# Sliding-window attention and a tanh-shrink layer: even key spans of V by DMA, odd ones copied by VectorE, GpSimd's casts for the third batch moved

## Chip, cores and metric

The kernel runs on one core of a Trainium2 chip. The metric is the device time of one execution in microseconds (us). A core has TensorE (PE in the profile), VectorE (DVE), ScalarE (ACT) and GpSimd (POOL), each with its own in-order instruction stream. SyncE (SP) here only issues DMAs. GpSimd issues DMAs as well, on a queue of its own.

## What is computed

Attention over a causal window of 64 keys, for 8 batches of 8 heads with 576 positions and head size 64, and then one layer with the activation h - tanh(h). The reference, cut down:

```python
scores = scale * np.matmul(q, k.transpose(0, 1, 3, 2))     # q, k, v: (8, 8, 576, 64), float32
rel = pos[:, None] - pos[None, :]
mask = (rel >= 0) & (rel < 64)
scores = np.where(mask, scores, -1000000000.0)
attn = softmax(scores)
x = (attn @ v).transpose(0, 2, 1, 3).reshape(4608, 512)
h = x @ w_in                                               # (512, 2048)
out = (h - np.tanh(h)) @ w_out                             # (2048, 512)
```

## The kernel before

**The two halves of the work.** The 4608 tokens of the layer are taken in nine chunks of 512. For each chunk c and each of 16 tiles m of the hidden size, `hp_mm` does four matmuls with `w_in` (L383) and a tanh on ScalarE (L388), `g_sub` the subtraction on VectorE (L395, into `gT`), and `yp_mm` the matmuls with `w_out` (L407); `y_out` copies the result (L412) and stores it from SP's queue (L414). `hp_mm` for chunk 0 starts with three tiles together, first for the half of `xT` that comes first (`split`), then for the other.

**Attention.** It is taken by pairs of heads: g = 4 b + pr, with batch b and pair pr, so 32 steps g. For each g: cast q and k to bf16 (`cast`, L85), transpose them on TensorE (`tr_rows` L269, later `tr` L249), copy them out of PSUM (L83 on ScalarE, L85 on VectorE), multiply (`tile_scores` L288, later `scores` L316), exponentiate (L291, L318), mask, multiply with V (`tile_pv` L304, later `pv` L332), and normalize (L308/L310, L339/L343). `tile_scores` masks in two ways: with "hide" it adds a large negative number by two matmuls (L276) in front of each of its two groups; with "mask" VectorE multiplies the exponentials by zero or one (L295). `x_tr` transposes the result into `xT`, from which `hp_mm` reads.

**V and its windows.** A query span of 64 tokens needs its own 64 keys and the 64 before. So `vw` holds, for each span j of nine, 128 rows: rows 64 to 127 are the keys of span j, rows 0 to 63 those of span j - 1. There are two such buffers, for even and odd batches. V is loaded to `vall`, cast into `vb` (`cast_v`, L85; 72 partitions of eight tokens), and from `vb` spread over partitions by DMA. Two ways are used: `keys_v` (L165) brings 64 rows of one span, 65 KB, and then the lower half is a copy of the upper half one span on, `shift_v`; `windows_v` (L150) brings all 128 rows, 130 KB. Before the change batches 0, 1 and 2 use nine `keys_v`, some issued by GpSimd (G) and some by SP (Y), and two VectorE copies `shift_dve` of 64 x 2080 elements (L171). Batches 3 and 4 use `windows_v`, the later ones `keys_v` and DMA.

**Order.** The order on every engine is written out by hand. A prologue does batch 0's attention. Then a loop over steps h issues the layer's instructions of step h (the table `OPS`), and after them whatever was put at this step by `at(h, ...)`, so `at(39, f)` places f at step 39. `cast_pair(g, eng)` casts k and q of g on the engine eng; `VALUES[b]` has the steps of batch b's casts of V and of its windows. Loads of q, k, V and the weights are issued by GpSimd, in the order of its stream: after the windows of batch 2 (step 23) come `w_out` in two halves and q, k and V of batch 3 whole. The DMAs of GpSimd use eight completion semaphores in turn, and each instruction that issues one waits for the DMA that had its semaphore before.

Of the kernel before, what the change touches and what calls it, by code (L numbers as in the profile page):

```python
# [15 lines left out]
def kernel(  # L16
# [9 lines left out]
    nc = tc.nc  # L26
    B, H, S, D = q.shape
    NP = H // 2
    NJ = S // 64
# [32 lines left out]
    mask = ps[:, 5, 448:480].bitcast(BF16)  # L62
    hide = const.tile([128, 2, 64], BF16, name="hide")
# [7 lines left out]
    vw = [const.tile([128, NJ, H, D + 1], BF16, name=f"vw{i}") for i in range(2)]  # L71
# [74 lines left out]
    def windows_v(b, j, eng):  # L146
        if j == 0:
            keys_v(b, 0, eng)
        else:
            eng.dma_start(out=vw[b % 2][:, j].rearrange("p h c -> p (h c)"),  # L150
                          in_=vb[8 * j - 8:8 * j + 8].rearrange("p e h c -> p e (h c)"))
# [7 lines left out]
    def cast_v(b, pr, eng=nc.gpsimd):  # L159
        move(eng, vb[:, :, 2 * pr:2 * pr + 2, 0:D].rearrange("p e h d -> p h e d"),  # L160
             stage.pop((b, pr, "v")).rearrange("p h (e d) -> p h e d", d=D))

    def keys_v(b, j, eng=nc.sync):

        eng.dma_start(out=vw[b % 2][64:128, j].rearrange("p h c -> p (h c)"),  # L165
                      in_=vb[8 * j:8 * j + 8].rearrange("p e h c -> p e (h c)"))

    def shift_v(b, j0, j1, eng=nc.sync):
        lo, hi = vw[b % 2][0:64, j0 + 1:j1 + 1], vw[b % 2][64:128, j0:j1]
        if eng is nc.vector:  # L170
            eng.tensor_copy(lo, hi)  # L171
        else:
            eng.dma_start(out=lo.rearrange("p j h c -> p (j h c)"), in_=hi.rearrange("p j h c -> p (j h c)"))
# [5 lines left out]
    def load_w_in(i):  # L179
        nc.gpsimd.dma_start(out=w_in_sb[i], in_=w_in_r[:, :, 1024 * i:1024 * i + 1024])  # L180

    def w_in_tile(ki, m):
        i = m // 8
        f = 512 * (m // 4 % 2) + m % 4
        return w_in_sb[i][:, ki, f:f + 4 * 127 + 1:4]
# [38 lines left out]
    def chunk_tile(c):  # L224
        if c not in xT:
            xT[c] = xt_pool.tile([128, WPC, 2, 128], BF16, tag="xT", name="xT")
        return xT[c]
# [7 lines left out]
    def tr_heads(g, which, bank, eng):  # L235

        src = stage.pop((g, which))
        tp = ps[:, bank, :].bitcast(BF16)[:, 0:E * P].rearrange("c (e p) -> c e p", e=E)
        for e in range(E):
            for h in range(2):  # L240
                nc.tensor.transpose(tp[64 * h:64 * h + 64, e, :], src[:, h, D * e:D * e + D], ident[:P, :P])
        o = qs[g % 2] if which == "q" else kT[g % NK][:, 64:]
        move(eng, o.rearrange("c (p e) -> c p e", e=E), tp.rearrange("c e p -> c p e"))
# [29 lines left out]
    def hides(grp, banks):  # L273
        n = GROUPS[grp][1]
        for h in range(2):
            nc.tensor.matmul(ps[:, banks[h], 0:64 * n], ident, hide[:, h].unsqueeze(1).to_broadcast([128, n, 64]),  # L276
                             start=True, stop=False)

    def tile_scores(g, grp, banks, how="hide"):

        j0, n = GROUPS[grp]
        if how == "hide":
            hides(grp, banks)
        for i in range(n):
            j = j0 + i
            for h in range(2):
                r = slice(64 * h, 64 * h + 64)
                nc.tensor.matmul(ps[:, banks[h], 64 * i:64 * i + 64], kT[g % NK][r, 64 * j:64 * j + 128],  # L288
                                 qs[g % 2][r, 64 * j:64 * j + 64], start=how == "mask", stop=how == "mask" or i == n - 1)
        o = PT[g % NPT][:, j0:j0 + n].rearrange("p j (h t) -> p h j t", h=2)  # L290
        nc.scalar.activation(o, pair_of(banks)[:, :, 0:64 * n].rearrange("p h (j t) -> p h j t", t=64),  # L291
                             ACT.Exp, scale=scale)
        if how == "mask":
            p = PT[g % NPT][:, j0:j0 + n].rearrange("p j (h t) -> p (j h) t", h=2)
            nc.vector.tensor_tensor(p, p, mask_sb.unsqueeze(1).to_broadcast([128, 2 * n, 64]), ALU.mult)  # L295
# [78 lines left out]
    def hp_bank(c, m):  # L374
        return H0_BANKS[m] if c == 0 else (m + 2) % 3 if c == 1 else m % 2

    def hp_mm(c, ms, split):

        outs = [ps[:, hp_bank(c, m), :] for m in ms]
        for kis in ((0, 2), (1, 3)) if split else ((0, 1, 2, 3),):  # L380
            for m, hp in zip(ms, outs):
                for ki in kis:
                    nc.tensor.matmul(hp, w_in_tile(ki, m),  # L383
                                     chunk_tile(c)[:, :, ki % 2, 64 * (ki // 2):64 * (ki // 2) + 64],
                                     start=(ki == 0), stop=(ki == 3))
        for m, hp in zip(ms, outs):
            th = sm_pool.tile([128, TOK], F32, tag="th", name="th")
            nc.scalar.activation(th, hp, ACT.Tanh)  # L388
            HID[c, m] = hp, th
# [51 lines left out]
    def at(h, fn, *args):  # L441
        items.setdefault(h, []).append((fn, args))
# [3 lines left out]
        c, m = [OPS[i][1:] for i in range(h) if OPS.get(i, "-")[0] == "h"][-1]  # L446
        nc.gpsimd.tensor_copy(tick, gT[c][0:1, m, 0:1])  # L447

    def shift_dve(b, *js):
        for j in js:  # L450
            shift_v(b, j, j + 4, nc.vector)

    V, A, G, Y = nc.vector, nc.scalar, nc.gpsimd, nc.sync

# [19 lines left out]
        cast_v(0, pr, V)  # L474
    tile_scores(0, 0, (0, 1))
    tile_scores(0, 1, (4, 5))
    for j, eng in enumerate((G, G, G, Y, G, Y, G, Y, G)):
        keys_v(0, j, eng)
    load_w_in(0)
    for pr in range(NP):  # L480
        load_v(1, pr)
# [17 lines left out]
    tile_scores(2, 0, (0, 1), "mask")  # L499
    tile_scores(2, 1, (4, 5), "mask")  # L500
    tr_heads(3, "q", 3, A)
    shift_dve(0, 0, 4)
    hides(0, (0, 1))
    hides(1, (4, 5))
    tile_scores(3, 0, (0, 1), "hidden")
# [16 lines left out]

    at(0, lambda: nc.vector.memset(vw[1][0:64, 0], 0.0))
    at(0, lambda: nc.vector.memset(qT[1], 0.0))
    for pr, h in enumerate((0, 0, 1, 3)):
        at(h, cast_v, 1, pr, V)
    at(9, lambda: [keys_v(1, j, (G, Y)[j % 2]) for j in range(NJ)])
    at(5, cast_pair, 4, V)
    at(9, cast_pair, 5, V)
    for pr in range(NP):  # L530
        at(9, load_v, 2, pr)
# [2 lines left out]
        at(9, load, g, "q", G)  # L534
    at(16, cast_pair, 6, V)
    at(16, cast_pair, 7, V)
    at(18, shift_dve, 1, 0, 4)
    for g, t, ka, qa, a, b, eng in ((4, (10, 11, 13, 14), 6, 7, (4, 5), (6, 7), V),
                                    (5, (13, 14, 16, 17), 2, 3, (4, 5), (6, 7), V),
                                    (6, (17, 18, 20, 22), 2, 3, (4, 5), (4, 5), A),  # L540
                                    (7, (20, 22, 24, 26), 3, 3, (4, 5), (4, 5), A),
                                    (8, (31, 32, 34, 36), 3, 5, (4, 5), (4, 5), A),
                                    (9, (37, 38, 42, 44), 3, 6, (4, 5), (4, 5), A)):
        at(t[0], tr_rows, g, "k", ka, eng)
        at(t[1], tr_rows, g, "q", qa, A)
        at(t[2], tile_scores, g, 0, a, "hide" if g < 8 else "mask")
        at(t[3], tile_scores, g, 1, b, "hide" if g < 8 else "mask")
    for pr in range(NP):
        at(22 + 2 * pr, tile_pv, 4 + pr, (6, 7))
    at(27, x_tr, 1, 0, 0, 4, 3, A)  # L550
# [1 line left out]
    at(30, x_tr, 1, 1, 0, 4, 7, V)  # L552
    at(30, x_tr, 1, 1, 4, 9, 4, A)
    at(21, lambda: [cast_v(2, pr) for pr in range(NP)])
    at(21, cast_pair, 8, G)
    at(23, lambda: [keys_v(2, j, (G, Y)[j % 2]) for j in range(NJ)])
    at(33, cast_pair, 9, V)
    at(23, load_w_out, 0)
    at(23, load_w_out, 1)
    at(23, load_all, 3, "q")  # L560
    at(23, load_all, 3, "k")
    at(23, load_v_all, 3)
    at(44, cast_pair, 10, G)
    at(50, cast_pair, 11, G)
    at(39, shift_dve, 2, 0, 4)
    at(44, tile_pv, 8, (6, 7))
    at(48, tile_pv, 9, (6, 7))
    at(53, x_tr, 2, 0, 0, 4, 6, V)
    at(55, x_tr, 2, 0, 4, 9, 7, A)
    at(76, x_tr, 2, 1, 0, 4, 3, V)  # L570
# [2 lines left out]
    LOADS = {4: (75, 77, 79), 5: (106, 109, 102), 6: (140, 144, 126), 7: (0, 0, 158)}  # L573
    STEPS = {2: (0, 0, 49, 57), 3: (72, 79, 86, 93), 4: (100, 107, 114, 121), 5: (128, 135, 142, 149)}
    TURNS = {13: (97, 3, 99, 3), 15: (110, 4, 111, 3)}
    VALUES = {3: (66, 1, 71), 4: (88, 1, 93), 5: (110, 2, 120), 6: (132, 5, 150), 7: (168, 2, 175)}
    for g in range(2 * NP + 2, B * NP):
        b, pr = divmod(g, NP)
        a = STEPS[b][pr] if b in STEPS else 8 * g - 36
# [28 lines left out]
        if b > 2:  # L608
            cv, cs, ky = VALUES[b]
            at(cv + cs * pr, cast_v, b, pr)  # L610
# [16 lines left out]
    for h in range(32 * NC + 64):  # L627
        op = OPS.get(h)
        if op and op[0] == "h":
            c, m = op[1:]  # L630
            if c == 0 and m == 0:
                hp_mm(c, (0, 1, 2), True)
            elif c > 0 or m > 2:
                hp_mm(c, (m,), m == 0)
        elif op == ("y", NC - 1, M - 4):
            y_last()
        elif op and op[1:] < (NC - 1, M - 4):
            yp_mm(*op[1:])
            if op[2] % 4 == 3:
                y_out(op[1], op[2] // 4)  # L640
        for fn, args in items.pop(h, []):
            fn(*args)
        if op and op[0] == "h":
            g_sub(*op[1:])
# [30 lines left out]
```

## Time and profile before

| | us |
|---|---|
| median of 4 runs | 337.04 (336.88 to 337.54) |
| the profiled execution | 340.34 |
| its span, first to last instruction | 338.6 |
| TensorE / VectorE / ScalarE / GpSimd busy | 319.8 / 198.5 / 184.0 / 118.6 |
| DMA moved | 40.68 MB, 120 GB/s on average |

In the groups of instructions, each line has the source line, engine, operation, what is written from what, shapes and count, then busy time in us and the mean of one in ns, and the idle time of its engine before these instructions with what ended it:

```profile
L395 DVE TENSOR_TENSOR gT<-ps,th 128x512 bf16<-128x512 f32 x144 | 98.4, 689 | 72.7 <-ACT th L388 71.5
...
L85 POOL COPY vb<-vall 72x1024 bf16<-72x1024 bf16 x24 | 24.7, 1052 | 35.4 <-DMA vall<-in_v_dram 25.8
...
L85 POOL COPY kb<-kall 96x768 bf16<-96x768 bf16 x23 | 19.8, 859 | 2.5 <-DMA kall<-in_k_dram 2.5
```

A timeline line has the start in us, the duration in us, the engine, source line, operation and count, and in brackets the idle time before it and its releaser. A line of waits has who waited for whom: us in total, how many times, the longest. A row of the table of windows has the stretch and its length, the busy us (and number of instructions) of PE, PE's weight loads, DVE, ACT and POOL, the granted clock of TensorE as a share of full speed, the DMA engines' busy share, and GB/s.

### The profile page before, as it was taken

The numbers are of one execution on the slowest core, as the hardware profiler recorded it, in microseconds if no ns is written. First come the engines' busy times: TensorE is split into PE (matmuls) and PEld (weight loads), VectorE is DVE, ScalarE is ACT, GpSimd is POOL, SyncE is SP. The second block draws the span as 40 slices with busy tenths as digits, with TensorE's granted clock in tenths as the row PEclk, the third lists the DMA queues.
The fourth block names the chain that finished last, engine by engine and source line by source line (L and its number), as shares of the span: only waits on it lengthen the run. The fifth ranks groups of instructions, "written<-read, shape, count | busy, mean of one in ns | idle before, by whom it ended". The sixth has DMA issues, their size and how long they took to land.

```text
span 338.6 us, 6275 instructions
## 1 busy us (share of the span) xinstructions
PE 319.8 (94%) x2439; PEld 176.6 (52%) x2439; DVE 198.5 (59%) x335; ACT 184.0 (54%) x337; POOL 118.6 (35%) x173
## 2 busy tenths in 40 slices
PE   6769999899987999999999999999999999999996
PEld 2544565555544655555565555555555444444444
DVE  4586697983254767666676766677665444443300
ACT  3534778683553676666566666655554444444411
POOL 8837499603940725730823585400000000000000
PEclk9598999999997999999999999999999999999999
DMA  8999998996599189648693996787213200100022
GB/s 160 162 179 191 171 155 123 174 203 133 86 174 182 13 147 180 135 80 163 110 172 92 172 179 137 139 195 166 57 57 68 71 33 31 62 33 31 31 75 83
DMA packets 47318, 40.68 MB, mean 120 GB/s; under 512 B 18728, under 2 KB 40680, under 8 KB 47096
## 3 DMA queue, kind: packets, MB, share of 16 engines
q0 software_dynamic: 21536, 19.73, 39.5%
q1 hardware_dynamic: 25544, 20.25, 23.4%
q8 instruction: 19, 0.31, 0.4%
q10 hardware_dynamic: 208, 0.29, 0.3%
q14 instruction: 11, 0.09, 0.1%
HBM read 36.70 MB, written 10.62 MB: 140 GB/s over the span
## 4 chain that ended last, share of the span: by engine, by line
PE 69%; DMA 12%; DVE 7%; POOL 6%; ACT 3%; issue 2%; POOLq 0%; DVEq 0%
PE ps L407 33%; PE ps L383 27%; DMA vw<-vb 4%; DMA qall<-in_q_dram 3%; DMA wi<-in_moe_w_in_dram 3%; PE ps L332 3%; PE ps L316 3%; DVE xs L343 2%; PE ps L249 2%; DMA kall<-in_k_dram 2%; POOL vall L143 1%; DVE gT L395 1%; DVE qt L85 1%; POOL kall L96 1%; POOL qall L96 1%
## 5 line engine op out<-in xcount | busy, mean ns | idle before, releaser
L383 PE MATMUL ps<-xT,wi 128*128 128x512 bf16 x576 | 149.2, 384 | 3.4 <-DMA wi<-in_moe_w_in_dram 1.6
L407 PE MATMUL ps<-w_out_sb,gT 128*128 128x512 bf16 x560 | 141.5, 380 | 0.0
L395 DVE TENSOR_TENSOR gT<-ps,th 128x512 bf16<-128x512 f32 x144 | 98.4, 689 | 72.7 <-ACT th L388 71.5
L388 ACT ACTIVATE th<-ps 128x512 f32<-128x512 f32 x144 | 85.9, 598 | 88.6 <-PE ps L383 84.9
L383 PEld LDWEIGHTS <-wi 128*128 128x128 bf16 x576 | 60.9, 114 | 49.8 <-issue 5.9
L407 PEld LDWEIGHTS <-gT 128*128 128x128 bf16 x560 | 52.4, 98 | 53.0 <-issue 1.1
L318 ACT ACTIVATE pt<-ps 128x384 bf16<-128x384 f32 x66 | 32.3, 489 | 23.8 <-PE ps L316 23.8
L85 POOL COPY vb<-vall 72x1024 bf16<-72x1024 bf16 x24 | 24.7, 1052 | 35.4 <-DMA vall<-in_v_dram 25.8
L343 DVE TENSOR_TENSOR xs<-ps,rc 64x576 bf16<-64x576 f32 x44 | 33.2, 755 | 1.1
L412 ACT ACTIVATE ysb<-ps 128x512 f32<-128x512 f32 x35 | 21.0, 599 | 18.9 <-PE ps L407 18.8
L85 DVE COPY qt<-ps 64x576 bf16<-64x576 bf16 x18 | 13.7, 760 | 24.1 <-ACT qt L83 24.1
L332 PEld LDWEIGHTS <-pt 128*128 128x128 bf16 x198 | 16.5, 98 | 18.8 <-issue 3.5
L85 POOL COPY qb<-qall 96x768 bf16<-96x768 bf16 x23 | 19.7, 857 | 17.8 <-DVE gT L395 10.7
L332 PE MATMUL ps<-vw,pt 128*128 128x130 bf16 x198 | 22.2, 220 | 3.8 <-DMA vw<-vb 3.4
L316 PE MATMUL ps<-qt,kt 128*128 128x128 bf16 x198 | 22.0, 220 | 0.0
L85 POOL COPY kb<-kall 96x768 bf16<-96x768 bf16 x23 | 19.8, 859 | 2.5 <-DMA kall<-in_k_dram 2.5
L316 PEld LDWEIGHTS <-kt 128*128 128x128 bf16 x198 | 15.6, 99 | 9.2 <-issue 0.8
L322 DVE TENSOR_TENSOR pt<-pt,ps 128x1152 bf16<-128x1152 bf16 x22 | 16.4, 745 | 0.8 <-ACT pt L318 0.8
L83 ACT ACTIVATE kt<-ps 128x576 bf16<-128x576 bf16 x22 | 14.4, 654 | 1.9 <-PE ps L249 1.6
L291 ACT ACTIVATE pt<-ps 128x640 bf16<-128x640 f32 (+1 forms) x20 | 12.5, 647 | 2.9 <-PE ps L288 2.9
L447 POOL COPY tick<-gT 1x1 bf16<-1x1 bf16 x14 | 2.5, 179 | 28.5 <-DVE gT L395 21.3
L165 POOL DMA_DIRECT2D vw<-vb x17 | 10.1, 600 | 6.2 <-DMA wi<-in_moe_w_in_dram 2.9
(76 smaller groups left out, 214.9 us busy)
## 6 DMA issues: line engine op xcount, KB each, us to landing
out_dram<-ysb SPq DMA_DIRECT2D x35, 256.0 KB
vall<-in_v_dram POOLq DMA_DIRECT2D x5, 576.0 KB, 12.0
vw<-vb SPq DMA_DIRECT2D x39, 65.0 KB
qall<-in_q_dram POOLq DMA_DIRECT2D x4, 576.0 KB, 11.9
kall<-in_k_dram POOLq DMA_DIRECT2D x4, 576.0 KB, 10.6
kall<-in_k_dram POOLq DMA_DIRECT2D x15, 144.0 KB, 6.0
qall<-in_q_dram POOLq DMA_DIRECT2D x15, 144.0 KB, 5.7
wi<-in_moe_w_in_dram POOLq DMA_DIRECT2D x2, 1024.0 KB, 10.6
```

The lines of the kernel that those rows point to most:

```text
L83: nc.scalar.activation(o, i, ACT.Copy)
L85: eng.tensor_copy(o, i)
L316: nc.tensor.matmul(sp[:, i, :], kT[g % NK][:, 64 * j:64 * j + 128], qT[g % NR][:, :, 64 * j:64 * j + 64], start=True, stop=True)
L318: nc.scalar.activation(PT[g % NPT][:, 3 * grp:3 * grp + 3, :], sp, ACT.Exp, scale=scale)
L322: nc.vector.tensor_tensor(p, p, mask.unsqueeze(1).to_broadcast([128, 2 * NJ, 64]), ALU.mult)
L332: nc.tensor.matmul(ps[:, 5 + grp, 130 * i:130 * i + 130], PT[g % NPT][:, j, :], vw[b % 2][:, j, 2 * pr:2 * pr + 2, :], start=True, stop=True)
L343: nc.vector.tensor_tensor(xo[r, :, :, pr, :], ov[r, :, :, h, 0:D], rc[r].to_broadcast([64, 3, 3, 64]), ALU.mult)
L383: nc.tensor.matmul(hp, w_in_tile(ki, m), chunk_tile(c)[:, :, ki % 2, 64 * (ki // 2):64 * (ki // 2) + 64], start=(ki == 0), stop=(ki == 3))
L388: nc.scalar.activation(th, hp, ACT.Tanh)
L395: nc.vector.tensor_tensor(gT[c][:, m, :], hp, th, ALU.subtract)
L407: nc.tensor.matmul(yp, gT[c][:, m, s * 128:(s + 1) * 128], w_out_sb[:, m, :], start=(m == 0), stop=(m == M - 1))
L412: nc.scalar.activation(ysb, ps[:, yp_bank(c, s), :], ACT.Copy)
```

## The change

Batches 0, 1 and 2 get V differently. The five even spans j = 0, 2, 4, 6, 8 come whole by DMA with `windows_v` (j = 0 needs only its upper half). The odd spans are copied by VectorE from their neighbours: the lower half of j is the upper half of j - 1, and the upper half of j is the lower half of j + 1 (`odd_windows`). A batch so has five DMAs instead of nine, with the same bytes, and two VectorE copies of 4 x 520 elements (for batch 2, three copies: one of 4 x 520 and two of 2 x 520, the last a step later). Batch 2's five DMAs are all issued by GpSimd.

k and q of g = 8, 10 and 11, which GpSimd cast, are cast by VectorE (8 and 11) and ScalarE (10). The transposes and scores of g = 8 and 9 come one to three steps later, their products with V one step later, g = 9's cast three steps later, and the casts of batch 1's V are spread over the steps 0, 1, 3, 5. g = 5's scores are masked by VectorE's multiplication instead of by matmuls. Batch 3's casts of V are at the steps 68 to 71 and its windows at 72, instead of 66 to 69 and 71. `hp_mm` starts chunk 0 with two tiles together instead of three.

```diff
-    def shift_dve(b, *js):
-        for j in js:
-            shift_v(b, j, j + 4, nc.vector)
+    def odd_windows(b, half, j0=1, n=4):
+
+        lo, hi = vw[b % 2][0:64], vw[b % 2][64:128]
+        at_j = slice(j0, j0 + 2 * n - 1, 2)
+        if half == 0:
+            nc.vector.tensor_copy(lo[:, at_j], hi[:, j0 - 1:j0 + 2 * n - 2:2])
+        else:
+            nc.vector.tensor_copy(hi[:, at_j], lo[:, j0 + 1:j0 + 2 * n:2])
+
+    def even_windows(b, *engs):
+
+        for j, eng in zip((0, 4, 2, 8, 6), engs):
+            windows_v(b, j, eng)
...
-    for j, eng in enumerate((G, G, G, Y, G, Y, G, Y, G)):
-        keys_v(0, j, eng)
+    for j, eng in ((8, Y), (0, G), (2, G), (4, G), (6, G)):
+        windows_v(0, j, eng)
...
-    shift_dve(0, 0, 4)
+    odd_windows(0, 0)
+    odd_windows(0, 1)
...
-    for pr, h in enumerate((0, 0, 1, 3)):
+    for pr, h in enumerate((0, 1, 3, 5)):
         at(h, cast_v, 1, pr, V)
-    at(9, lambda: [keys_v(1, j, (G, Y)[j % 2]) for j in range(NJ)])
-    at(5, cast_pair, 4, V)
+    at(9, even_windows, 1, G, Y, G, Y, G)
+    at(6, cast_pair, 4, V)
...
-    at(18, shift_dve, 1, 0, 4)
+    at(18, odd_windows, 1, 0)
+    at(18, odd_windows, 1, 1)
...
-                                    (8, (31, 32, 34, 36), 3, 5, (4, 5), (4, 5), A),
-                                    (9, (37, 38, 42, 44), 3, 6, (4, 5), (4, 5), A)):
+                                    (8, (34, 35, 37, 39), 3, 5, (4, 5), (4, 5), A),
+                                    (9, (38, 39, 42, 44), 3, 6, (4, 5), (4, 5), A)):
...
-        at(t[2], tile_scores, g, 0, a, "hide" if g < 8 else "mask")
-        at(t[3], tile_scores, g, 1, b, "hide" if g < 8 else "mask")
+        at(t[2], tile_scores, g, 0, a, "hide" if g in (4, 6, 7) else "mask")
+        at(t[3], tile_scores, g, 1, b, "hide" if g in (4, 6, 7) else "mask")
...
-    at(21, cast_pair, 8, G)
-    at(23, lambda: [keys_v(2, j, (G, Y)[j % 2]) for j in range(NJ)])
-    at(33, cast_pair, 9, V)
+    at(31, cast_pair, 8, V)
+    at(23, even_windows, 2, G, G, G, G, G)
+    at(36, cast_pair, 9, V)
...
-    at(44, cast_pair, 10, G)
-    at(50, cast_pair, 11, G)
-    at(39, shift_dve, 2, 0, 4)
-    at(44, tile_pv, 8, (6, 7))
-    at(48, tile_pv, 9, (6, 7))
+    at(46, cast_pair, 10, A)
+    at(53, cast_pair, 11, V)
+    at(39, odd_windows, 2, 0)
+    at(39, odd_windows, 2, 1, 1, 2)
+    at(40, odd_windows, 2, 1, 5, 2)
+    at(45, tile_pv, 8, (6, 7))
+    at(49, tile_pv, 9, (6, 7))
...
-    VALUES = {3: (66, 1, 71), 4: (88, 1, 93), 5: (110, 2, 120), 6: (132, 5, 150), 7: (168, 2, 175)}
+    VALUES = {3: (68, 1, 72), 4: (88, 1, 93), 5: (110, 2, 120), 6: (132, 5, 150), 7: (168, 2, 175)}
...
-                hp_mm(c, (0, 1, 2), True)
-            elif c > 0 or m > 2:
+                hp_mm(c, (0, 1), True)
+            elif c > 0 or m > 1:
```

## Prediction, made before the changed kernel was run

> **What bounds the kernel now.** I read the page first, then TensorE's waits, then the table of windows, then GpSimd's timeline backwards from the longest wait.
>
> ```profile
> PE 319.8 (94%) x2439; PEld 176.6 (52%) x2439; DVE 198.5 (59%) x335; ACT 184.0 (54%) x337; POOL 118.6 (35%) x173
> ...
> PEclk9598999999997999999999999999999999999999
> ```
>
> TensorE is the bound, 319.8 of 338.6 us, so only what it waits for, and its clock, can give time. Each digit of the clock row is a fortieth, 8.5 us: after the start there is one dip, the 7 of the slice from 101.6 us.
>
> ```profile
> PE ps L332 <- DMA vw<-vb: 3.4, 1, 3.4
> PE ps L383 <- DMA wi<-in_moe_w_in_dram: 1.6, 1, 1.6
> ...
> PE ps L383 <- DVE gT L395: 1.4, 3, 0.8
> ...
> PE ps L269 <- POOL kb L85: 0.7, 1, 0.7
> ```
>
> The longest wait (99.9 + 0.2 to 103.47 us) is the product with V of batch 3, held by one of the transfers that fill `vw`. It costs twice: the clock after it is granted at 0.59 for 4 us, a loss of 0.41 x 4 = 1.6 us.
>
> ```profile
> 100.00:104.00 4.00, 0.62 (x6) 0.34 (x4) 1.67 (x3) 0.66 (x2) 0.00 (x0) 0.98 1.22 257
> 104.00:108.00 4.00, 4.00 (x19) 2.02 (x18) 2.86 (x4) 1.52 (x3) 0.00 (x0) 0.59 1.02 201
> ```
>
> So 3.4 + 1.6 = 5.0 us hang on when batch 3's V reaches `vw`. GpSimd's timeline tells why it is late:
>
> ```profile
> 36.84 0.55 POOL L165 DMA_DIRECT2D vw<-vb  x1 [2.92 <-DMA wi<-in_moe_w_in_dram]
> 38.10 0.55 POOL L165 DMA_DIRECT2D vw<-vb  x1 [0.70 <-DMA kall<-in_k_dram]
> 39.58 0.71 POOL L143 DMA_DIRECT2D vall<-in_v_dram  x1 [0.93 <-DMA qall<-in_q_dram]
> ...
> 47.97 4.03 POOL L85 COPY vb<-vall 72x1024 bf16<-72x1024 bf16 x4
> 51.94 0.82 POOL L85 COPY kb<-kall 96x768 bf16<-96x768 bf16 x1
> 52.71 0.82 POOL L85 COPY qb<-qall 96x768 bf16<-96x768 bf16 x1
> 53.48 2.92 POOL L165 DMA_DIRECT2D vw<-vb  x5
> 56.39 1.49 POOL L188 DMA_DIRECT2D w_out_sb<-in_moe_w_out_dram  x2
> ...
> 82.00 1.05 POOL L85 COPY vb<-vall 72x1024 bf16<-72x1024 bf16 x1 [5.67 <-DMA vall<-in_v_dram]
> 82.99 0.82 POOL L85 COPY kb<-kall 96x768 bf16<-96x768 bf16 x1
> 83.76 3.04 POOL L85 COPY vb<-vall 72x1024 bf16<-72x1024 bf16 x3
> ```
>
> V of batch 3 lands at 82.0. It is queued behind `w_out`, q and k, and these behind GpSimd's casts and window transfers. Meanwhile the DMA engines run half empty:
>
> ```profile
> 52.00:54.00 2.00, 1.34 (x15) 0.76 (x13) 0.95 (x3) 1.60 (x4) 2.00 (x3) 1.00 0.60 86
> 54.00:56.00 2.00, 1.90 (x23) 1.10 (x22) 1.22 (x3) 1.85 (x4) 2.00 (x5) 1.00 0.72 130
> 56.00:58.00 2.00, 2.00 (x23) 1.06 (x22) 1.30 (x4) 1.78 (x4) 2.00 (x4) 1.00 0.90 143
> 58.00:60.00 2.00, 2.00 (x15) 0.99 (x13) 1.96 (x4) 1.90 (x4) 2.00 (x3) 1.00 0.66 84
> ```
>
> The last column is GB/s: 111 on average over 8 us, where 66 to 76 us has 205. That is 8 x (205 - 111) / 205 = 3.7 us of transfer time lost.
>
> **Start (0 to 25 us).** Batch 0's windows: nine transfers of 65 KB become one of 65 and four of 130, so bytes are equal; GpSimd issues 4 instead of 6, 2 x 0.57 us less. In the program's list of waits its DMAs share eight completion semaphores in turn, so each waits for the one eight before it; the first `w_in` load at 14.16 waited 0.77 us so. Two DMAs fewer put it behind an earlier one (k of g=2, landed by 11.9): issue at 9.67 + 4 x 0.57 = 12.0. The transfers are in order, so only unused DMA time counts: 15 to 18 us has 159, 110 and 141 GB/s against about 190 later, 160 KB short, 0.85 us. TensorE waits 1.6 us for `w_in`; take 0.8 us gain (0 to 1.6). The odd copies need all even windows, so the first product with V can start only after the second copy, near 18.5 instead of 18.23; it is hidden, since `xT` is ready at 24.5 and its first half at 22.7. `hp_mm` with two tiles instead of three lets the first tanh start four matmuls earlier; nothing waits there but a 0.8 us wait for gT at 33.9; taken as 0.
>
> A rule against row: the Trainium skill (TensorE: Matmul & The Clock Gate, Part 1) has the clock halve after an idle window of about 3.4 us. The trace halves it after less: 1.6 us of waiting, with thin work before it, and 25 to 29 us is granted 0.57. By the rule a shorter wait removes that 1.7 us; by the row it may well stay, so I take 0.
>
> **GpSimd's queue (31 to 56 us).** The windows of batch 1 are 3 instead of 5 issues on GpSimd. In the row above the last two are held by the rotation until 36.84 and 38.10, and the V loads of batch 2 behind them until 39.58. With two fewer these loads stand two places further back: the first waits for `w_in`'s second half (36.8, less 0.8) and the last for the load that lands at 40.6, less 0.8. From there 8 issues x 0.64 = 5.1 us: about 45.0 instead of 47.97, 3.0 us (1 to 3). Then 4.0 us casts of V, no k and q casts (-1.54), five window issues (2.8): `w_out` is issued at about 52 instead of 56.4, 4.5 us earlier. The DMA time to be filled is 3.7 us, so V of batch 3 lands 3.5 us earlier, at 78.5 (2 to 4). A k cast no longer stands between its V casts (-0.8): all cast at 82.5 instead of 86.8. SP's half of batch 3's windows stands behind two stores of y, the second out at 83.6, whose time is TensorE's. So the windows come 3.2 us earlier, plus what TensorE gains.
>
> A rule that speaks against this: the Trainium skill (SBUF — State Buffer, SBUF: two separate sides) says a DMA issued by GpSimd cannot get its descriptors written while VectorE runs a two-port copy. Batch 2's windows all move to GpSimd. The row: 17 such issues take 551/571/957 ns (min, median, max), those five 0.56 to 0.64, and land after 3.5 to 4.0 us. By the row the move costs nothing; by the rule up to a copy (0.70) an issue, 3.5 us. I keep the row for the middle and 2 us for the range.
>
> **The compute engines (31 to 76 us).**
> - Batch 2's window copies on VectorE: two took 2.46 us beside GpSimd's k and q casts, the pair of batch 1 1.33 us without them. Without casts: -1.1 us. TensorE's waits there are 0.4 (gT, 62.8) and 0.3 us (xs, 65.1). The new copies have the same elements in runs of 520 with gaps; no row shows gaps. Bounds: as before, 0.70 each, or one element a cycle, by the 64x520 memset at 0.49, so 2.0 each. Runs are long and rows even: 0.7.
> - k and q of g=8 from GpSimd to VectorE: +0.70, in a VectorE idle of 1.8 us (54.8); TensorE's wait of 0.7 us for kb goes, and its next is for `xT` (53.0): 0.4 gained.
> - g=10 to ScalarE: two copies, nearest row 0.84 (96x768 from fp32), lower bound 0.65; +1.7 us in a stretch where ScalarE waits 1.4 and 0.5 us for TensorE. g=11 to VectorE: +0.70 at about 69 us, where VectorE is 97% busy; up to 0.7 lost.
> - g=5's mask by multiplication: four matmuls fewer (1152 columns; 512 take 0.216 us: -0.5 us on TensorE), 0.49 + 0.42 more on VectorE, ahead of gT and of the window copies, whose product with V follows at 44.3: up to 0.9 lost.
> - Steps of g=8, g=9, their products with V and the last cast of g=8: later by 1 to 3 steps, free as long as batch 2 is not what the end waits for.
>
> Sum for TensorE ahead of 100 us: 0.8 + 0.4 + 0.5 + 0.7 = 2.4, less a likely half of the added 0.7 + 0.9 + 0.5: about 1.4 us (-1 to 2.5).
>
> **The sum.** TensorE would reach the product at 100.1 - 1.4 = 98.7; the windows are there at 103.5 - 3.2 - 1.4 = 98.9. The wait is nearly gone and the clock stays: 4.6 + 1.6 = 6.2 us off the profiled execution, which took 340.3 us (span 338.6 and 1.7 around it): 334.1. The median of the runs is 337.0, 3.3 less. The only places where it can have lost less are such waits and clock dips, so I suppose that an ordinary run has some 2 to 3 of the 5.0 us. That gives 337.0 - 1.4 - 2.2 = 333.4.
>
> **Rivals.**
> 1. The stall stays: the last window on SP took 12.6 us in the chain (90.82 to 103.47) beside batch 4's k, q and V loads, which are issued right behind the windows (91.4 to 94.9) and so come earlier too. For: 201 to 257 GB/s there. Against: all shift alike. Only 1.4 us remain: 335.6. Chance 0.2.
> 2. The added VectorE and ScalarE work (3 us) lands on TensorE and eats the gain: within 0.2% of before, 337.0. For: VectorE 87% busy from 54 to 66 us. Against: TensorE had 3.4 us to spare before the stall. Chance 0.08.
> 3. Slower: the odd copies of batch 2 at step 39 block VectorE. All five even windows are on one queue; if GpSimd is not early, the last is issued at 54.8 and lands by the worst row (9.8 us) at 64.6, five us after the copies' turn at 59.6; gT stands behind them, and TensorE has two banks. It decides once the last even window lands after about 63, when more than the stall's 3.4 us is lost. Then 5.0 - 1.8 (the part of the stall an ordinary run has): about 340. Chance 0.12.
> The main case has 0.6.
>
> **Numbers.** Within 0.2% (0.7 us) is about what a measurement of this kernel cannot tell from no change. Faster 0.60 + 0.20 = 0.80, same 0.08, slower 0.12. The range goes from the full profile gain (337.0 - 6.4 = 330.6) to no change (337.0), which leaves out rival 3 and half of rival 2.
>
> **What would show it.** Right: batch 3's first V cast near 78.5 us, `w_out` issued near 52, 52 to 60 us near 200 GB/s, no wait of L332's product over 1 us, no 7 in the clock row, window copies of 0.7 us. Wrong: V cast of batch 3 still at 82 (the queue was not the cause); TensorE waiting for gT or xs between 55 and 80 us (rival 2); VectorE idle before the odd copies (rival 3).

## The result and the profile after

| | before | after |
|---|---|---|
| median of the runs side by side, us | 336.55 (56 runs, 333.9 to 340.98) | 334.40 (37 runs, 332.5 to 336.89) |
| ratio after / before | | 0.9948 [0.9933, 0.9962] |
| the profiled execution, us | 340.34 | 336.89 |
| its span | 338.6 | 335.2 |

By the ratio the change makes the kernel 0.52% faster, 1.75 us (1.3 to 2.3) of 336.55; the two medians are 2.15 us apart, inside that interval. The prediction took off 3.6 us. Both profiled executions are near the longest of their kernels' runs, so the difference of the two spans is not the gain; they show where time goes within each.

The page of after, its TensorE totals and clock row:

```profile
PE 318.1 (95%) x2435; PEld 176.5 (53%) x2435; DVE 199.3 (59%) x342; ACT 185.4 (55%) x339; POOL 110.9 (33%) x163
...
PEclk9569899999999999999999999999999999999999
```

The 7 at 101.6 us is gone. A new 8 stands in the fifth slice (33.5 to 41.9 us). The waits of TensorE in after (total us, how often, the longest):

```profile
PE ps L383 <- DMA wi<-in_moe_w_in_dram: 2.3, 2, 1.8
...
PE ps L383 <- DVE gT L395: 1.0, 2, 0.8
...
PE ps L407 <- ACT ysb L412: 0.3, 1, 0.3
```

The wait of L332's product for `vw`, 3.4 us before, is not in the list at all. The longest wait of the layer is now for the second half of `w_in`, 1.8 us. The table of windows of after confirms both stretches (columns as before: PE, PE's loads, DVE, ACT, POOL, clock, DMA share, GB/s):

```profile
36.00:38.00 2.00, 0.24 (x4) 0.13 (x2) 0.67 (x1) 0.98 (x2) 0.00 (x0) 1.00 1.31 243
...
40.00:42.00 2.00, 2.00 (x11) 1.02 (x10) 1.61 (x5) 1.67 (x4) 2.00 (x4) 0.50 0.94 147
...
52.00:54.00 2.00, 2.00 (x19) 1.09 (x17) 1.97 (x5) 1.67 (x4) 2.00 (x5) 1.00 0.76 62
54.00:56.00 2.00, 1.85 (x19) 1.15 (x19) 1.51 (x4) 1.33 (x4) 2.00 (x3) 1.00 0.93 164
56.00:58.00 2.00, 1.61 (x21) 0.86 (x19) 1.75 (x5) 2.00 (x5) 1.69 (x3) 1.00 0.86 145
58.00:60.00 2.00, 2.00 (x27) 1.33 (x26) 1.61 (x3) 1.72 (x4) 0.00 (x0) 1.00 1.08 168
100.00:104.00 4.00, 4.00 (x32) 2.24 (x29) 2.80 (x5) 3.16 (x7) 0.00 (x0) 1.00 1.09 184
104.00:108.00 4.00, 4.00 (x34) 2.39 (x33) 2.93 (x5) 2.19 (x5) 0.00 (x0) 1.00 0.56 119
```

At 100 to 108 us TensorE is now busy throughout at full clock. From 52 to 60 us the DMA engines move (62 + 164 + 145 + 168) / 4 = 135 GB/s instead of 111, not the 200 that the prediction hoped for. Between 36 and 38 us TensorE waits for `w_in`, and from 39.5 us on the clock is halved.

GpSimd's timeline of after, the lines that answer to the chain shown of before:

```profile
38.11 0.71 POOL L143 DMA_DIRECT2D vall<-in_v_dram  x1 [5.01 <-DMA wi<-in_moe_w_in_dram]
...
46.78 4.03 POOL L85 COPY vb<-vall 72x1024 bf16<-72x1024 bf16 x4
...
51.71 2.12 POOL L150 DMA_DIRECT2D vw<-vb  x4
53.79 1.49 POOL L188 DMA_DIRECT2D w_out_sb<-in_moe_w_out_dram  x2
...
80.21 4.04 POOL L85 COPY vb<-vall 72x1024 bf16<-72x1024 bf16 x4 [2.86 <-DMA vall<-in_v_dram]
84.54 0.60 POOL L165 DMA_DIRECT2D vw<-vb  x1 [0.30 <-POOL vb L85]
```

`w_out` is issued 2.6 us earlier than before (53.79 for 56.39), V of batch 3 lands 1.8 us earlier (80.21 for 82.0) and its windows start 2.6 us earlier (84.54 for 87.10), since no k cast lies between its four casts. But the first profile of before began late: in a second one (e5, below) the same three stand at 55.34, 80.84 and 85.94, and after is ahead of them by only 1.6, 0.6 and 1.4 us.

To see where TensorE gains or loses, I read from each trace when VectorE begins the subtraction (L395) of the first, ninth, 32nd and 39th tile of the layer, in us from the start of the span; the last column goes from the 39th tile to the last instruction. The first tile needs the first half of `w_in`, the ninth the second half; the 32nd comes after all of batches 1 and 2's work, the 39th after the product that stalled. Experiments are listed too, and told below.

| us | 1st tile | 9th | 32nd | 39th | 9th to 32nd | 32nd to 39th | 39th to end |
|---|---|---|---|---|---|---|---|
| before, first profile | 29.56 | 41.41 | 74.83 | 111.03 | 33.42 | 36.20 | 227.6 |
| before again (e5) | 27.04 | 40.36 | 73.77 | 105.22 | 33.41 | 31.45 | 227.6 |
| after | 27.82 | 41.30 | 75.80 | 106.80 | 34.50 | 31.00 | 228.4 |
| after, g=5 by matmuls (e4) | 26.73 | 41.44 | 74.33 | 105.66 | 32.89 | 31.33 | 228.4 |
| after, V first (e8) | 28.50 | 41.48 | 74.35 | 105.34 | 32.87 | 30.99 | 228.4 |
| before, V first (e3) | 25.95 | 39.39 | 72.97 | 103.96 | 33.58 | 30.99 | 227.6 |
| casts part alone (e2) | 26.82 | 40.28 | 72.78 | 104.54 | 32.50 | 31.76 | 227.8 |
| windows part alone (e1) | 26.95 | 39.00 | 75.03 | 106.02 | 36.03 | 30.99 | 228.1 |

Four things stand in it. The column from the 32nd to the 39th tile shows the stall: 36.20 - 31.00 = 5.2 us in the two profiles at hand. The column before it shows the work between: 34.50 in after, of which about 1.7 us is the half clock from 39.5 to 42.9 us (3.4 x 0.5), so 32.8 without it, against 33.4. The ninth tile starts between 39.0 and 41.6 us, with no order between kernels that have the old windows and those that have the new. And the last column shows a loss of 0.8 us behind the 39th tile, in each of the three profiles of after and its near kin. Of it 0.3 us comes with the casts part: the wait for ScalarE's copy of y (L412) in the list above, which before and e1 do not have. The other 0.5 us comes with the windows part, behind all work: from the end of the last copy (L425) to the last instruction it is 2.8 us in every profile with the old windows and 3.3 us in every one with the new, where SyncE runs out its last waits. Why, the runs do not show.

### The profile page after: what moved, and what is told of

Read it like the earlier page. It is cut to its first block, busy times and chain, and to the rows that moved or that the text cites. A ratio compares the mean times of both kernels' runs of the same rounds, so it can differ in the third digit from the quotient of the medians.

```text
span 335.2 us, 6239 instructions
## 1 busy us (share of the span) xinstructions
PE 318.1 (95%) x2435; PEld 176.5 (53%) x2435; DVE 199.3 (59%) x342; ACT 185.4 (55%) x339; POOL 110.9 (33%) x163
## 4 chain that ended last, share of the span: by engine, by line
PE 75%; DMA 9%; DVE 7%; ACT 4%; issue 2%; POOL 2%; POOLq 0%; DVEq 0%; ACTq 0%
PE ps L407 34%; PE ps L383 30%; DMA wi<-in_moe_w_in_dram 7%; PE ps L332 3%; PE ps L316 3%; DVE xs L343 2%; PE ps L249 2%; DMA kall<-in_k_dram 2%; DVE qt L85 2%; DVE gT L395 1%; ACT qt L83 1%; PE ps L422 1%; ACT pt L318 1%; POOL vall L143 1%; PE ps L349 1%
## 5 line engine op out<-in xcount | busy, mean ns | idle before, releaser
L395 DVE TENSOR_TENSOR gT<-ps,th 128x512 bf16<-128x512 f32 x144 | 98.5, 690 | 68.1 <-ACT th L388 66.7
L412 ACT ACTIVATE ysb<-ps 128x512 f32<-128x512 f32 x35 | 21.0, 600 | 18.9 <-PE ps L407 18.5
L85 POOL COPY qb<-qall 96x768 bf16<-96x768 bf16 x20 | 16.6, 832 | 25.5 <-DMA qall<-in_q_dram 25.5
L332 PEld LDWEIGHTS <-pt 128*128 128x128 bf16 x198 | 16.5, 98 | 15.3 <-DVE pt L322 0.8
L332 PE MATMUL ps<-vw,pt 128*128 128x130 bf16 x198 | 22.0, 220 | 0.4 <-DVE pt L322 0.4
L85 POOL COPY kb<-kall 96x768 bf16<-96x768 bf16 x20 | 16.6, 829 | 3.1 <-DMA kall<-in_k_dram 3.1
L96 POOL DMA_DIRECT2D qall<-in_q_dram x15 | 9.9, 660 | 7.5 <-DMA wi<-in_moe_w_in_dram 6.2
L83 ACT ACTIVATE qt<-ps 64x576 bf16<-64x576 bf16 x18 | 11.5, 638 | 1.0 <-PE ps L249 0.9
```

The source lines that it names most:

```text
L83: nc.scalar.activation(o, i, ACT.Copy)
L85: eng.tensor_copy(o, i)
L332: nc.tensor.matmul(ps[:, 5 + grp, 130 * i:130 * i + 130], PT[g % NPT][:, j, :], vw[b % 2][:, j, 2 * pr:2 * pr + 2, :], start=True, stop=True)
L395: nc.vector.tensor_tensor(gT[c][:, m, :], hp, th, ALU.subtract)
L412: nc.scalar.activation(ysb, ps[:, yp_bank(c, s), :], ACT.Copy)
```

## The experiments

The theory after the result: the gain is mostly the stall of batch 3's V, which GpSimd's freed queue takes away; of what TensorE was to gain ahead of it little came. Rivals: the new windows at the start bring the gain; or TensorE's gain was there and the work added to VectorE and ScalarE (g=5's mask, the casts) ate it. In these kernels only order, engine and way of transfer change.

### e1: the windows part alone

Before, with the even windows by DMA and the odd ones copied, all else as it was:

```diff
+    def odd_windows(b, half, j0=1, n=4):
...
-    for j, eng in enumerate((G, G, G, Y, G, Y, G, Y, G)):
-        keys_v(0, j, eng)
+    for j, eng in ((8, Y), (0, G), (2, G), (4, G), (6, G)):
+        windows_v(0, j, eng)
...
+    at(9, even_windows, 1, G, Y, G, Y, G)
+    at(18, odd_windows, 1, 0)
+    at(18, odd_windows, 1, 1)
+    at(23, even_windows, 2, G, G, G, G, G)
+    at(39, odd_windows, 2, 0)
+    at(39, odd_windows, 2, 1, 1, 2)
+    at(40, odd_windows, 2, 1, 5, 2)
```

> The kernel before with only the windows part: even spans by DMA, odd ones copied, batches 0 to 2; casts and steps stay. Queue theory (the time comes from batch 3's V reaching vw earlier): GpSimd's stream is shorter by the two issues and the rotation alone, about 1.2 us by the changed kernel's first V cast of batch 2 (46.78 for 47.97), so about 1 us faster than before (ratio 0.997), a wait on vw of about 2 us left in the profile. Engine theory (the gain is TensorE's own, from the copies and the earlier start): most of the change's gain is here, ratio 0.995 to 0.996, whatever the wait on vw does.

Measured: 0.9986 [0.9965, 1.0007] of before, no change that can be told, and less than either expectation. The profile has no stall of batch 3's V, but a new one, in VectorE's timeline of e1:

```profile
57.99 1.77 DVE L454 COPY vw<-vw 64x2080 bf16<-64x2080 bf16 x1 [1.64 <-DMA vw<-vb]
59.80 1.27 DVE L456 COPY vw<-vw 64x1040 bf16<-64x1040 bf16 x2
```

VectorE stands idle for 1.64 us until the last even window has landed, and then its copies take 1.77 and 1.27 us, beside GpSimd's k and q casts (56.83 to 60.4 us), the last of which is longer too, in GpSimd's timeline of e1:

```profile
58.37 0.84 POOL L85 COPY kb<-kall 96x768 bf16<-96x768 bf16 x1
59.14 1.31 POOL L85 COPY qb<-qall 96x768 bf16<-96x768 bf16 x1
```

In after, with no casts there, the same copies take 0.70 and 0.77 us, in VectorE's timeline of after:

```profile
60.92 0.70 DVE L454 COPY vw<-vw 64x2080 bf16<-64x2080 bf16 x1
61.65 0.77 DVE L456 COPY vw<-vw 64x1040 bf16<-64x1040 bf16 x2
```

In e1 TensorE's product with V (L304) waits 2.1 us for these copies, and the clock is halved from 61.9 to 65.3 us, another 1.7. The 9th-to-32nd column shows 36.03 - 33.42 = 2.6 us of it, net of what else moved. So in this execution the windows part alone is rival 3 of the prediction, at a smaller size: the old stall is gone and another stands in its place. It is one profile; how often ordinary runs have the new stall isn't shown.

### e2: the casts part alone

Before, with k and q of g = 8, 10, 11 off GpSimd and the steps of g = 8, 9 and of batch 3's casts of V later:

```diff
-    at(21, cast_pair, 8, G)
+    at(31, cast_pair, 8, V)
-    at(44, cast_pair, 10, G)
-    at(50, cast_pair, 11, G)
+    at(46, cast_pair, 10, A)
+    at(53, cast_pair, 11, V)
...
-    VALUES = {3: (66, 1, 71), 4: (88, 1, 93), 5: (110, 2, 120), 6: (132, 5, 150), 7: (168, 2, 175)}
+    VALUES = {3: (68, 1, 72), 4: (88, 1, 93), 5: (110, 2, 120), 6: (132, 5, 150), 7: (168, 2, 175)}
```

> The kernel before with only the casts of g=8, 10, 11 off GpSimd and the later steps (transposes, scores and products of g=8 and 9, V casts of batch 3); windows stay. Queue theory: w_out is issued 1.6 us earlier (two casts of 0.8) and no k cast stands between the V casts of batch 3 (0.8), so the windows of batch 3 come about 2 us earlier, the wait on vw shrinks from 3.4 to about 1 us; TensorE pays for the casts on ScalarE (up to 1 us): ratio 0.995 to 0.997. Engine theory: no gain or slower, 1.000 to 1.003, because ScalarE and VectorE have more to do.

Measured: 0.9959 [0.9935, 0.9984], within the expectation of the queue theory. By the middle of the interval this part alone has most of the gain; against the whole change (0.9948) the intervals overlap. `w_out` is issued at 54.11 and batch 3's casts of V begin at 79.74, close to after's 53.79 and 80.21. The wait for `vw` is 0.6 us in its profile, and the 9th-to-32nd stretch is the shortest of all, 32.50 us.

### e3: the stall alone

Before, with one thing changed: V of batch 3 is loaded ahead of its q and k, and cast at once.

```diff
+    at(23, load_v_all, 3)
     at(23, load_all, 3, "q")
     at(23, load_all, 3, "k")
-    at(23, load_v_all, 3)
...
-    VALUES = {3: (66, 1, 71), 4: (88, 1, 93), 5: (110, 2, 120), 6: (132, 5, 150), 7: (168, 2, 175)}
+    VALUES = {3: (64, 0, 71), 4: (88, 1, 93), 5: (110, 2, 120), 6: (132, 5, 150), 7: (168, 2, 175)}
```

> The kernel before with one thing moved: V of batch 3 is loaded ahead of q and k of batch 3, and cast ahead of them (casts of V at step 64). Nothing is taken from any engine. Queue theory: V lands near 76 us instead of 82, the windows start as soon as SP's two stores of y are issued (83.6), the wait on vw and the clock dip after it vanish, TensorE up to 100 us is as before; ordinary runs gain what the stall costs them, 2 to 3 us (ratio 0.991 to 0.994). Engine theory (ordinary runs have no such stall, it is a thing of the profiled execution): ratio 0.999 to 1.001.

Measured: 0.9962 [0.9941, 0.9983], 1.3 us (0.6 to 2.0), less than the 2 to 3 us of the one expectation and more than the nothing of the other. In GpSimd's timeline of e3 V of batch 3 is cast 9 us earlier than in the first profile of before, and its windows follow at 79.4:

```profile
73.00 4.04 POOL L85 COPY vb<-vall 72x1024 bf16<-72x1024 bf16 x4 [10.07 <-issue]
```

There is no wait for `vw`, 32nd to 39th tile takes 30.99, and the work up to there is as in before (33.58). So this is the stall's mean price over ordinary runs, with whatever the later q and k cost: about 1.3 us, not the 5.2 of the first profile.

### e4: g=5's mask by matmuls again

After, with one term taken back:

```diff
-        at(t[2], tile_scores, g, 0, a, "hide" if g in (4, 6, 7) else "mask")
-        at(t[3], tile_scores, g, 1, b, "hide" if g in (4, 6, 7) else "mask")
+        at(t[2], tile_scores, g, 0, a, "hide" if g < 8 else "mask")
+        at(t[3], tile_scores, g, 1, b, "hide" if g < 8 else "mask")
```

> The changed kernel with g=5 masked by matmuls again, as before. If VectorE's mask (0.9 us ahead of gT and the window copies near 41 to 45 us) is what costs TensorE its early lead, this is faster than the changed kernel by up to 0.9 us (ratio to before 0.992 to 0.994). If the lead is lost to the second half of w_in, which lands at 37.9 us, it changes nothing beyond the 0.5 us of the four matmuls (0.995 to 0.997).

Measured: 0.9943 [0.9923, 0.9963], the same as after. VectorE's extra multiplications neither cost nor bring anything that can be measured. In its profile TensorE, without the half clock, reaches the product with batch 3's V earlier than in after, and a rest of the stall is there:

```profile
PE ps L332 <- DMA vw<-vb: 0.2, 1, 0.2
```

### e5: before, a second profile

The kernel before, unchanged, profiled again, to see whether the stall is always there.

> The kernel before, unchanged, profiled once more. In the first profile the start was some 3 to 4 us later than in the profiles of four other kernels, one of which (V of batch 3 first) is the same up to 50 us. If the stall on vw belongs to ordinary executions, it is here again with 3 us or more. If it is tied to how the start falls, it is clearly smaller (0 to 2 us) and there is no clock dip after it; the 1.3 us that V first gained say about that.

Measured: one run, 334.51 us. TensorE's waits in e5 have the stall's row, ten times smaller:

```profile
PE ps L332 <- DMA vw<-vb: 0.3, 1, 0.3
```

Of the 5.81 us that separate the two profiles at the 39th tile, 1.1 lie ahead of the product and 36.20 - 31.45 = 4.75 are the stall and the clock behind it. V of batch 3 is cast 1.2 us earlier than in the first profile (80.84), but TensorE is 1.1 us earlier too, so that is not the difference. The chain of work that ended last tells it (start, duration, what):

```profile
89.55 9.74 DMA vw<-vb
99.28 0.04 issue
99.33 0.27 PE ps L332 x2
```

The transfer of the last window takes 9.74 us, in the first profile 12.61 (90.82 to 103.43): 2.9 of the 3.1 us by which the wait is shorter. It runs where the DMA engines are full (197 and 246 GB/s in the two halves of 96 to 104 us in e5, 147 and 257 in the first profile), and how long it takes differs between executions of the same kernel. So the stall is a race, lost in one execution and nearly won in another.

### e6: GpSimd casts g = 10 and 11 again, but late

After, with the two casts back on GpSimd, held by a one-element copy that waits for the layer's step, so that they don't start early:

```diff
-    at(46, cast_pair, 10, A)
-    at(53, cast_pair, 11, V)
+    at(42, pace, 42)
+    at(42, cast_pair, 10, G)
+    at(46, pace, 46)
+    at(46, cast_pair, 11, G)
```

> The changed kernel, with k and q of g=10 and 11 cast by GpSimd, as before the change, but held back by two ticks (steps 42 and 46) until VectorE's window copies are done; GpSimd has nothing else to do from 57.7 to 73.7 us. If the casts on ScalarE and VectorE cost TensorE its time at 64 to 71 us (it lost 1.9 us there between two tiles), this wins about 1 us over the changed kernel: ratio to before 0.991 to 0.993. If that stretch is bound by something else, it is as the changed kernel: 0.994 to 0.996.

Measured: 0.9986 [0.9964, 1.0007]: the gain of after is gone, which neither expectation allowed for. GpSimd's timeline of e6, then VectorE's:

```profile
60.99 0.82 POOL L85 COPY kb<-kall 96x768 bf16<-96x768 bf16 x1
61.76 0.81 POOL L85 COPY qb<-qall 96x768 bf16<-96x768 bf16 x1
```

```profile
61.52 1.33 DVE L295 TENSOR_TENSOR pt<-pt,mask_sb 128x512 bf16<-128x512 bf16 x1
```

The mask's multiplication, 0.43 us elsewhere, takes 1.33 beside the casts. The normalization is late behind it, TensorE's next product waits 1.8 us for `xs`, and the clock is half from 65.5 to 68.9. So at these steps the casts cost more on GpSimd than on the engines that took them over: taking them off is a gain there, not a price. That speaks against the second rival.

### e7: e6 with g=5 by matmuls

> The paced casts and g=5 masked by matmuls together, on the changed kernel. If both costs are real and separate, the best so far: 0.989 to 0.992. If neither is, 0.994 to 0.996.

Measured: 0.9974 [0.9947, 1.0000], outside both expectations; its edit is e4's on top of e6. The interval overlaps e6's, so this doesn't tell more than e4 did; the 1.33 us multiplication and the 1.8 us wait for `xs` are in its profile too.

### e8: V first, on top of after

After, with e3's edit: the load of V ahead of q and k, `3: (64, 0, 72)`.

> The changed kernel with V of batch 3 loaded and cast ahead of q and k of batch 3. The profile of the changed kernel has no wait on vw any more, so by the queue theory this finds nothing to gain: 0.994 to 0.996. If ordinary runs of the changed kernel still wait for V of batch 3, it gains up to 1.3 us: 0.991.

Measured: 0.9948 [0.9924, 0.9973], exactly after's ratio. V is cast at 76.83 instead of 80.21, and that is worth nothing that can be measured: in ordinary runs after has no stall left that would be worth removing. It also gives a profile of after's middle without the half clock: 32.87 us from the 9th to the 32nd tile.

### e9 and e10: the second half of w_in earlier

The wait for `w_in` is the largest left. In e9, after with its second half loaded before V of batch 1, and what depends on that V pushed back:

```diff
-    for pr, h in enumerate((0, 1, 3, 5)):
+    for pr, h in enumerate((13, 13, 14, 14)):
         at(h, cast_v, 1, pr, V)
-    at(9, even_windows, 1, G, Y, G, Y, G)
+    at(14, even_windows, 1, G, Y, G, Y, G)
...
-        at(9, load_v, 2, pr)
+        at(14, load_v, 2, pr)
...
-        at(9, load, g, "k", G)
-        at(9, load, g, "q", G)
+        at(14, load, g, "k", G)
+        at(14, load, g, "q", G)
```

> The changed kernel with the second half of w_in loaded ahead of V of batch 1, and batch 1's V cast, its windows and the loads behind them moved to steps 13 and 14. In eight profiles TensorE's ninth tile starts when that half lands (34.8 to 37.9 us) and whatever lead there was before is gone; in the changed kernel it waits 1.8 us and the clock is halved for 3.4 us after. If this is what eats TensorE's early lead, the wait goes, tile 9 starts about 2 us earlier, and the time falls by up to 2 us against the changed kernel (ratio to before 0.989 to 0.992). If the transfers behind it (V of batch 1, q and k of g=6, 7) only take its place, the ratio stays at 0.994 to 0.997, and a wait for V's windows or for k appears near 40 to 46 us.

Measured: 1.0040 [1.0024, 1.0056], slower than before. The ninth tile starts at 38.24, 3 us earlier than in after, as meant. Then the lead is lost. VectorE's timeline of e9, and TensorE's:

```profile
42.99 0.70 DVE L454 COPY vw<-vw 64x2080 bf16<-64x2080 bf16 x1 [3.74 <-DMA vw<-vb]
```

```profile
44.47 0.47 PE L304 MATMUL ps<-vw,pt 128*64 128x65 bf16 x18 [3.10 <-DVE vw L456]
```

Batch 1's windows land late, TensorE waits 3.1 us for them and has half the clock from 45.8 us. The expectation of a gain failed. V of batch 1 now stands behind the second half of `w_in`: its last two loads are issued at 24.15 us instead of 16.2, after GpSimd has waited 5.65 us for the semaphore of `w_in`'s first half, its last two casts run at 34.57 instead of 29.4 and 30.3, and its windows are issued from 35.3 instead of 30.7. From 16 to 36 us the DMA engines move 158 to 212 GB/s throughout, so the transfer that is brought forward takes its time from another that is needed as well.

e10 is e9 with e4's and e8's edits as well.

> The same with g=5 masked by matmuls and with V of batch 3 loaded first, so that nothing behind the moved loads can bring the stall on vw back: the best version if the pieces add up, ratio 0.987 to 0.991; 0.994 if the lead is lost elsewhere again.

Measured: 1.0019 [0.9997, 1.0041], with the same 3.1 us wait. No kernel that I tried is faster than after by more than the intervals.

## Why the prediction was right and too large

The direction, the median (334.4, inside the range) and the mechanism of the stall held; the size did not. 3.6 us were forecast as 1.4 for TensorE and 2.2 for the stall. Measured are 1.75, of which e3 puts 1.3 on the stall.

**The stall's share of an ordinary run: mis-sized.** "An ordinary run has some 2 to 3 of the 5.0 us" was a guess from one profile and four times, and the sum took 2.2. e5 has 0.3 us of wait and a full clock, e3 gives 1.3 us (0.6 to 2.0) on average. The profile of before had caught an execution with the whole stall. What the stall costs in that execution was right: 3.2 + 1.6 = 4.8 us off the profile, 5.2 measured between 32nd and 39th tile, the clock's part with it (1.00 from 100 to 108 us in after).

**The sum for TensorE, "0.8 + 0.4 + 0.5 + 0.7 = 2.4 ... about 1.4 us": the step that failed**, and in it the start.
- "Take 0.8 us gain": nothing came. `w_in` is issued earlier as forecast (13.26 us in after, 11.99 to 12.82 in five others with the new windows and the old order of loads, for 13.78 to 14.57 in four profiles with the old windows), but the first matmul of the layer starts at 25.2 us on average with the new and 24.3 with the old (spread 23.4 to 26.4). The DMA time that I counted as unused was used: from 14 to 18 us the six profiles have 162 to 210 GB/s, the four 150 to 159. But it did not turn into an earlier landing. From the landing ahead of it on GpSimd's queue to its own, `w_in` took 6.0 to 9.2 us with the new windows and 5.2 to 7.4 with the old; which transfers took its share, the runs don't tell apart. The second half of `w_in` follows the first: its issue (26.52 in after) stands behind a load that waits 6.25 us for the semaphore of the first. So it landed no earlier either, and the ninth tile waits for it, which I had not followed: in after 1.76 us.
- The odd copies let the first product with V start at 19.3, not the forecast 18.5 (18.2 before).
- The compute engines: from 33.4 to 32.8 or 32.9 us between the 9th and 32nd tile where the clock is full (e4, e8, and after less its 1.7), 0.5 us. That is within what the prediction summed for them, 0.4 + 0.5 + 0.7 less 1.05 = 0.55. The interval of 1.75 less 1.3 is wide (about -0.4 to 1.3), so the 0.5 rests on the traces. e2 has it too, without the new windows.
- Behind 100 us the sum had nothing, and there 0.8 us is lost (0.3 + 0.5, the last column of the table). Stall 1.3, compute 0.5, start 0, less 0.8 make 1.0, for 1.75 measured. That is inside the intervals (the stall's alone is 0.7 to either side), but the account does not close: some 0.7 us of the gain has no place in it.

**The clock at the start, taken as 0.** The half clock of 25 to 29 us in the first profile of before followed a wait of 1.64 us for `w_in`. In after that wait is 0.57 us and the clock there is full; in e5, with the kernel unchanged, there is no wait and no dip. So it belonged to one execution, and leaving it out of the sum was right.

**GpSimd's queue: right in kind, half in size at most.** The V loads of batch 2 could not start before `w_in`'s second half landed: 38.11, where I had taken 36. So its casts begin 1.2 us earlier (46.78), not 3.0, and against e5 (46.93) only 0.15. Over the six and four profiles the mean is 46.1 for 46.9. From there on the sum held: 46.78 to 53.79 is 7.0 us, forecast 7, where both profiles of before have 8.4. V of batch 3 lands 26.4 us after `w_out` is issued, before 25.6: the DMA engines gave back 0.8, and 1.8 us are left of the 3.5. The k cast between the V casts gave its 0.8. Together 2.6 us instead of 4.3 (1.4 against e5), and it was enough, though not by far: no wait in after's profile, 0.2 us in e4's, and e8's 3.4 us more bring nothing.

**The rule against the change**, that VectorE's copies keep GpSimd from writing a DMA's descriptors: the row was right for batch 2, whose four windows issue in 2.12 us in after, 0.53 each. But VectorE has no copy from SBUF to SBUF in that time, so this did not test the rule. Where it has, the rule shows. Two of batch 1's windows in GpSimd's timeline of after, then VectorE's copies:

```profile
31.61 1.49 POOL L150 DMA_DIRECT2D vw<-vb  x2
```

```profile
32.36 0.35 DVE L85 COPY kb<-kall 96x768 bf16<-96x768 bf16 x1
32.62 0.35 DVE L85 COPY qb<-qall 96x768 bf16<-96x768 bf16 x1
```

The second issue lies over both copies and takes 0.94 us, the first 0.56. So the price is 0.4 us here, less than the copies' own 0.7.

**Copies, casts, mask: right.** Window copies take 0.70 us; g=10's on ScalarE 0.83 each (0.84 taken); g=5's mask costs nothing (e4).

**The rivals.** 1, the stall stays: no (e8), but for the 0.2 us of e4. 2, added work eats the gain: no; e6 says that GpSimd was the dearer place for the casts. 3, the odd copies wait for the last window: not in after, but in e1, where VectorE waits 1.64 us and TensorE 2.1. The windows part needs the casts part: with GpSimd free of casts the windows come on time and the copies run undisturbed. The casts part does not need the windows: e2 has 0.9959 alone, and whether the windows add anything to it the intervals cannot tell.

What stays open, beside the 0.7 us: in how many executions of after the half clock at 40 us appears. It is in one of three profiles of after and its near kin, and would be worth 1.7 us.

## What to carry to other kernels

A wait in one profile that ends with the last of several transfers can be a race: before it is priced at its full length, look at a second profile of the same kernel, or remove only that wait and time the rest. A transfer issued earlier need not land earlier: `w_in` was issued about 1 us sooner here and landed no sooner. Ask which later wait takes back what the first one gave. Casts that an idle GpSimd takes are not free when VectorE works beside them (e6: 0.9986 for 0.9948). And compare the stretch behind the change too: 0.8 us was lost there, in work that the change does not touch.

## What the runs showed of the hardware

- VectorE and GpSimd slow each other. Beside GpSimd's casts a bf16 copy of 64x2080 took 1.77 us instead of 0.70, and a bf16 mask multiplication 1.33 instead of 0.43, while the casts took 0.81 to 0.85 and one 1.31 instead of 0.82. The Trainium skill (SBUF — State Buffer, SBUF: two separate sides) calls it an exclusive lock on a shared port pair, held for a whole instruction; the 0.90 and 1.07 us added are somewhat more than one cast. GpSimd's issue of a DMA suffers too: 0.94 us beside two of VectorE's copies, 0.56 without (after).
- Waits shorter than 3.4 us can halve the clock for 3.4 us: 1.64 us in before, 1.76 in after, 1.8 in e6, 2.1 in e1. But 2.15 us in e4 (35.2 to 37.4 us) and 1.86 in e8 (24.5 to 26.4 us) did not. The windows of e4 show it, with 1.00 in the column before the last two where after had 0.50:

```profile
35.00:37.00 2.00, 0.22 (x6) 0.07 (x2) 0.69 (x1) 1.08 (x3) 0.00 (x0) 1.00 1.26 227
...
39.00:41.00 2.00, 2.00 (x27) 1.25 (x26) 0.71 (x2) 1.91 (x5) 1.37 (x3) 1.00 0.93 147
```

  The Trainium skill (TensorE: Matmul & The Clock Gate, Part 1) says the window in which activity is watched runs freely, and that the moment at which the clock rises depends on where in it the first matmul lands. If the same holds for a gap, that would explain it; no run here shows where the windows lie.
- Transfers vary by themselves. The first layer tile came between 26.0 and 29.6 us in profiles with the same loads up to there (e3, e5, before), and the same window's transfer took 9.74 and 12.61 us.
